# A fused attention and S4 convolution kernel on one core: a new order of work, loads cut into single DMAs, spectra copied whole out of PSUM

## The chip, the core and the metric

The kernel runs on one core of one Trainium2 chip. The metric is the device time of one execution in microseconds (us). Each kernel is timed in several executions and the median is reported; one further execution is profiled. The core has a matrix engine (TensorE; PE in the profile, its weight loads PEld), a vector engine (DVE), an activation engine (ACT), a general engine (POOL) and a sync engine (SP), which issues nearly all of the DMAs here. Each engine works through its own list of instructions in order and waits, where it must, on semaphores that the others raise.

## The reference

Two independent computations share one launch, and their outputs are put side by side.

```
# A: sliding-window attention, S = 2048, D = 576, H = 32 heads of Dh = 18, window W = 256
qkv = x @ wqkv;  q, k, v = split into heads
scores = einsum("bhqd,bhkd->bhqk", q, k) * Dh ** -0.5
mask = (i - j >= 0) & (i - j < W)
p = softmax(where(mask, scores, -1e9))
a = (p @ v, heads concatenated) @ wo
# B: S4 convolution, L = 2048, D = 576 channels, N = 128 states
dt = exp(log_dt);  logdA = dt * (A_re + 1j * A_im);  dB = dt * B
K[d, l] = real(sum_n C[d, n] * exp(logdA[d, n] * l) * dB[d, n])
y = irfft(rfft(pad(u)) * rfft(pad(K)))[:L] + u * Dskip
out = concatenate([a, y], axis=-1)
```

## The kernel before

**Stages.** The work is given to the engines by hand, in four stages that `build` runs one after the other: `front` (loads, scales, the first value and query tiles), `tables` (the taps K of the convolution, beside the rest of the query, key and value projection), `first` (the attention's first groups beside the last taps) and `rest` (attention, convolution and output projection, mixed).

**The order is a table.** `PLAN` holds one string a stage. Each letter names a stream, a Python generator that emits one step of its work when its letter comes up. A letter with a digit emits the work that an earlier step left behind: an evacuation from PSUM, a product, a store. Nothing reorders the steps afterwards, so the position of a letter in the string is the place of those instructions in their engine's list. The letters that matter below:

- `P`: the projection. `G`, `M`, `N`, `R`, `X`: phases, magnitudes, sines, products on POOL and taps; `X4` stores the spectrum of the taps, tile `kst`, to DRAM (`gk`).
- `s`: one step of the pass over the scores for each row's maximum. There are 16 groups of heads and queries (four head groups by four chunks of 512 queries) with 16 such steps in each. A step is 8 matmuls (L844, L852) into a PSUM pair, which a maximum on DVE (`s2`, L878) empties. At the end of a group the maxima are transposed on PE, scaled on DVE, and stored by SP into the query tile as an extra row (`s4`, L871).
- `a`: one score step (L914, L927), ten a group; `a1` is its exponential on ACT (L932), which empties the pair. `v`: one step of the product with the values (L952), ten a group, into the separate pair `po`; `v1` evacuates that, and `n`, `n3`, `n1`, `n6`, `n4` normalise it (DVE, POOL, ACT, POOL) and store it in `od` (SP, L999).
- `k`: load of a tile of spectra of input and taps (`xk`, L672). `c`: 24 steps that transform it (L684) into two PSUM pairs at once. `c1` copies out of these on ACT (L692), `c2` multiplies on DVE (L699), `c3` adds and subtracts on POOL (L704, L705). `d`: the inverse transform (L716), `d1` its copy (L723), `d4` its store. `f`: reload (`hp`, L766). `e`: the last transform (L777). `L`: the loads of Q, K and V of a later group.
- `l`: the output projection's weights and their common scale. The scale goes through DRAM: DVE takes the maximum `om` (L1028), SP stores it (`omx`, L1030) and reads it back over all partitions (`orow`, L1032), and DVE goes on from that (L1034). `w`: the output projection in four chunks (L191 with `woh`); each chunk first reloads its part of `od` into `oh` and `ol`, of which there is one buffer.

**PSUM.** Besides `po`, three pairs of banks (`ring0` to `ring2`) serve every step. The string `SLOTS` says, allocation by allocation in the order of PE's steps, which of the three pairs the step takes. A pair can be taken again only when whatever reads it has read it.

**The spectra step before.** ACT copies the input half of each pair (192 of 384 columns) into `X`. DVE then multiplies `X` with the taps' half, which it reads from the PSUM pairs themselves. So both pairs are held until both products are done.

**DMAs on SP.** SP issues in order, and a DMA that has to wait holds up all behind it. There are eight DMA semaphores in turn, so that a DMA also waits for the one eight places earlier.

## Time and profile before

| | us |
|---|---|
| three timed executions | 870.95, 874.90, 877.46 |
| median | 874.9 |
| profiled execution, its own time | 871.51 |
| its span, first to last instruction | 869.7 |
| busy in the span: PE, DVE, ACT, POOL | 714.5, 599.3, 526.7, 377.8 |
| mean granted clock of PE | 0.928 of full speed |

In the trace the first matmul of the tables starts at 58 us, the first of the attention at 398 us, the first spectra step at 444 us, and the last matmul ends near 866 us. A busy PE is not a PE at its peak, since the ends of matmuls are modelled; what counts is where it stands idle, who ended that idle time, and where the granted clock is at half.

### The profile page before, as it was taken

To read this page: it belongs to the slowest core of one execution; us is meant where nothing else is said; L and a number is where in the kernel's file an instruction comes from. 1 tells how busy PE (TensorE), PEld (TensorE's weight loads), DVE (VectorE), ACT (ScalarE), POOL (GpSimd) and SP (SyncE) were. 2 spreads that over 40 slices of the span, in tenths; PEclk is the share of its full clock that TensorE was granted. 3 is DMA by queue.
4 is the path that set the end of the run, shared out by engine and by line. 5 is a ranking of instruction groups with operands and counts; after the bars stand their busy time and mean duration, and the time that the engine had idled before them with its cause. 6 is when DMAs were issued, how large, how long until landed. Compare 5 with 4: busy or idle time off the path is not lost. (4 is left out here: it accounts for less than half of the span.)

```text
span 869.7 us, 29448 instructions
## 1 busy us (share of the span) xinstructions
PE 714.5 (82%) x12954; PEld 414.7 (48%) x12954; DVE 599.3 (69%) x798; ACT 526.7 (61%) x709; POOL 377.8 (43%) x295
## 2 busy tenths in 40 slices
PE   3675967999889888896887789958998998889977
PEld 2421434456345644464534445425554544457655
DVE  6866887887987787776757798657786779751010
ACT  3247676678777867672455567636676676665421
POOL 2266867766687755565013424312243052432020
PEclk9885969999999999895889999979999999999998
DMA  9795261546347755459457866848549584746843
GB/s 314 266 233 133 63 161 35 142 97 162 83 104 196 150 131 157 100 157 249 100 189 229 268 197 209 212 122 243 180 146 276 170 260 153 216 130 183 245 137 133
DMA packets 211040, 150.74 MB, mean 173 GB/s; under 512 B 102698, under 2 KB 191530, under 8 KB 210656
## 3 DMA queue, kind: packets, MB, share of 16 engines
q1 hardware_dynamic: 208896, 144.87, 59.4%
q0 software_dynamic: 2016, 3.99, 1.5%
q8 instruction: 101, 1.65, 0.8%
q14 instruction: 27, 0.22, 0.1%
HBM read 83.57 MB, written 65.11 MB: 171 GB/s over the span
## 5 line engine op out<-in xcount | busy, mean ns | idle before, releaser
L878 DVE TENSOR_REDUCE m<-ring 128x2 f32<-128x640 f32 (+4 forms) x256 | 186.6, 779 | 52.0 <-PE ring L852 47.9
L932 ACT ACTIVATE P<-ring,esc 128x1024 f32<-128x1024 f32 (+2 forms) x160 | 167.7, 1060 | 83.1 <-PE ring L927 77.0
L559 POOL TENSOR_TENSOR m<-A,tr 128x1024 f32<-128x1024 f32 x72 | 143.9, 2018 | 77.5 <-DVE m L565 66.1
L844 PE MATMUL ring<-K,Q 54*64 54x320 f16 (+4 forms) x1024 | 81.1, 316 | 28.5 <-DMA K<-kz 9.2
L952 PE MATMUL po<-P,V 64*32 64x320 f32 (+4 forms) x2816 | 99.4, 358 | 5.2 <-issue 5.2
L704 POOL TENSOR_TENSOR Y<-t,t 128x384 f32<-128x384 f32 x24 | 24.0, 1001 | 137.5 <-DVE t L699 128.6
L986 POOL TENSOR_TENSOR osb<-osb,T 128x1024 f32<-128x1024 f32 x16 | 37.8, 2363 | 100.4 <-DVE T L981 74.9
L844 PEld LDWEIGHTS <-Q 54*64 54x64 f16 x1024 | 44.0, 108 | 73.8 <-issue 66.8
L914 PE MATMUL ring<-Q,K 55*64 55x320 f16 (+4 forms) x1408 | 65.9, 266 | 15.5 <-ACT P L932 7.0
L191 PE MATMUL pp<-xh,wh 128*128 128x512 f16 x180 | 49.4, 406 | 17.5 <-ACT vst L378 8.2
L994 POOL TENSOR_TENSOR oh<-osb,oh 128x1024 f16<-128x1024 f32 x16 | 34.1, 2131 | 67.5 <-ACT oh L990 67.4
L699 DVE TENSOR_TENSOR t<-X,ring 128x768 f32<-128x768 f32 x48 | 43.5, 946 | 23.8 <-ACT X L692 16.7
L191 PEld LDWEIGHTS <-wh 128*128 128x128 f16 x324 | 32.0, 102 | 55.5 <-issue 18.3
L914 PEld LDWEIGHTS <-K 55*64 55x64 f16 x1408 | 33.3, 108 | 48.2 <-issue 41.2
L565 DVE TENSOR_TENSOR m<-m,m 128x1024 f32<-128x1024 f32 x36 | 53.0, 1472 | 4.8 <-POOL m L559 4.7
L852 PE MATMUL ring<-sm,idb 64*64 64x128 bf16 x896 | 55.1, 222 | 0.6 <-issue 0.6
L588 PE MATMUL ring<-Q,m 128*32 128x64 f32 x2304 | 42.6, 231 | 15.4 <-DVE m L565 13.4
L952 PEld LDWEIGHTS po<-P,V 64*32 64x32 f32 x2816 | 37.8, 106 | 34.0 <-issue 24.1
L588 PEld LDWEIGHTS ring<-Q,m 128*32 128x32 f32 x2304 | 37.0, 117 | 28.7 <-issue 13.0
L191 PE MATMUL pp<-xh,wl 128*128 128x512 f16 x180 | 50.6, 417 | 0.0
L977 DVE STREAM_TRANSPOSE T<-osb 128x1024 f32<-128x1024 f32 x16 | 19.8, 1236 | 42.2 <-ACT osb L962 42.1
L540 POOL TENSOR_TENSOR tr<-tr,mab 128x768 f32<-128x768 f32 x18 | 33.6, 1868 | 30.4 <-ACT tr L535 30.3
(159 smaller groups left out, 1535.6 us busy)
## 6 DMA issues: line engine op xcount, KB each, us to landing
gx<-ust SPq DMA_DIRECT2D x16, 576.0 KB
gk<-kst SPq DMA_DIRECT2D x18, 512.0 KB
xk<-gx SPq DMA_DIRECT2D x24, 384.0 KB
xk<-gk SPq DMA_DIRECT2D x24, 384.0 KB
h<-ho SPq DMA_DIRECT2D x48, 192.0 KB
hp<-h SPq DMA_DIRECT2D x12, 768.0 KB
Q<-qz SPq DMA_DIRECT2D x16, 512.0 KB
K<-kz SPq DMA_DIRECT2D x16, 512.0 KB
```

Of the source, the lines that this page charges most:

```text
L191: self.nc.tensor.matmul(ps, u, v, start=(i == 0), stop=(i == len(ops) - 1))
L559: tt(m[part], A[:, ch, a0:a0 + 8].unsqueeze(3).to_broadcast(sh), tr[:, ch, part, 0:8].unsqueeze(2).to_broadcast(sh), op=OP.mult)
L565: self.nc.vector.tensor_tensor(m[0], m[0], m[1], op=OP.add)
L588: nc.tensor.matmul(kp[32 * st:32 * st + 32, j, :], m[:, ch, 32 * term:32 * term + 32], Q[:, ch, term, :], start=(term == 0), stop=(term == ...
L699: tt(tm, X, pi[i][:, :, 192:384].unsqueeze(2).to_broadcast(sh), op=OP.mult)
L844: nc.tensor.matmul(ps[z:z + 64, b, :n], d["Q"][rr, 2 * b + pp, 64 * qb:64 * qb + 64], d["K"][rr, 2 * b + pp, k0:k1], start=True, stop=Fals ...
L852: nc.tensor.matmul(out, self.idb[rr], self.sm[rr], start=False, stop=True, skip_group_check=True)
L878: self.nc.vector.tensor_reduce(out, x, axis=AX.X, op=OP.max)
L914: nc.tensor.matmul(ps[z:z + 64, b, off:off + w], d["K"][rr, 2 * b + pp, kc:kc + 64], d["Q"][rr, 2 * b + pp, q0:q0 + w], start=(k == 0), st ...
L932: nc.scalar.activation(P[:, :, lo:hi], ps[:, :, lo:hi], AF.Exp, scale=self.esc)
L952: nc.tensor.matmul(po[32 * p:32 * p + 32, z, q0:q0 + w], V[64 * z:64 * z + 64, kb * 76 + 19 * p:kb * 76 + 19 * p + 32], P[p % 2][64 * z:64 ...
L986: nc.gpsimd.tensor_tensor(osb, osb, rb, op=OP.mult)
```

## The change

**The tables of the order.** The strings for `tables`, `first` and `rest` and the string `SLOTS` are all new; `front` is unchanged. The four stages and the arithmetic of all steps except the spectra stay as they are. The number of steps differs only where a DMA is now a step of its own. One line of many:

```
     "rest":
-        "ava1s2ss6ss2s4sss2s2sss2s2ss2sss2s2sss2s2vvsass2aa1a1ss2s2ksvs2sks2aa1ass2ava1a1cc1cc2avv1c1c3a1vvva"
...
+        "ass2s2ss4kskssss2vvs2sasa1a1kvvs2s2vss2s2as2sa1s2s2Laas2s2ssaka1vv1a1a1s2s2vcc1saa1avvLacaka1svs6c2s"
...
 SLOTS = (
-    "0121202102102102102210210120210210210210120121020210120210210201201021020121012021021021021201210201"
...
+    "0122201202112010120102121012012101201020210210120020121021010202012012010201021020211012021010020120"
...
```

**Loads and stores as single DMAs.** The store of the taps' spectrum becomes two DMAs of 256 KB instead of one of 512 KB, each a step of its own. The load of a spectra tile (two DMAs), of a group's Q, K and V (three or four DMAs) and of `hp` (now two halves) were one step each; now every DMA is one step, and other DMAs can stand between them. In all 30 more DMAs are issued.

**Spectra copied whole.** ACT copies all 384 columns of both pairs into a larger `X`, and DVE takes both factors of its products from `X` in SBUF. The pairs are free after ACT's copies.

```
+    def each(self, fn):
+        left, cur = [2], self.cur
+
+        def done():
+            left[0] -= 1
+            if not left[0]:
+                self.cur = cur
+                fn()
         return done
...
-        end = self.both("4", (kst,), lambda: nc.sync.dma_start(gv[:, :, GC * q:GC * q + GC], kst.rearrange("p l s j -> p l (s j)")))
+        def store(l):
+            nc.sync.dma_start(gv[:, l:l + 16, GC * q:GC * q + GC], kst[:, l:l + 16].rearrange("p l s j -> p l (s j)"))
+
+        def stored():
+            for l in (0, 16):
+                self.post("4", (kst,), lambda l=l: store(l))
+        end = self.each(stored)
...
         for m, g in enumerate((self.gx, self.gk)):
+            yield "SP", ()
             nc.sync.dma_start(x[:, :, m], g[8 * t:8 * t + 8, :, :, 192 * ch:192 * ch + 192]
...
         def first():
-            X = fy.tile(sh, F32, name="X")
+            X = fy.tile([128, 2, 2, 384], F32, name="X")
             for i in range(2):
-                nc.scalar.activation(X[:, :, i], pi[i][:, :, :192], AF.Copy)
-            self.post("2", (X, *pi), lambda: second(X))
+                nc.scalar.activation(X[:, i], pi[i][:, :, :384], AF.Copy)
+            self.post("2", (X,), lambda: second(X))
...
             for i, tm in enumerate((t1, t2)):
-                tt(tm, X, pi[i][:, :, 192:384].unsqueeze(2).to_broadcast(sh), op=OP.mult)
+                tt(tm, X[:, :, :, :192].rearrange("p i s j -> p s i j"),
+                   X[:, i, :, 192:].unsqueeze(2).to_broadcast(sh), op=OP.mult)
...
-            self.nc.sync.dma_start(self.hp[m], hv[:, 8 * k:8 * k + 8, 192 * ch:192 * ch + 192])
+            for r in (0, 4):
+                if r:
+                    yield "SP", ()
+                self.nc.sync.dma_start(self.hp[m][:, r:r + 4], hv[:, 8 * k + r:8 * k + r + 4, 192 * ch:192 * ch + 192])
...
         for i in range(3, 16):
-            yield "SP", (), lambda: i - 3 in self.osb
-            self.load(i)
+            for part in self.parts(i):
+                yield "SP", (), lambda: i - 3 in self.osb
+                part()
```

Three places where the order changes follow. The line numbers of the changed kernel are up to 27 higher (L878 is L904 there, L1032 is L1059).

The first place is SP's list between the store of the weights' maximum (`omx`) and its reading back (`orow`), in `rest`. Before:

```order
L1030 DMA omx<-om 128x1
L814 DMA Q_4402<-qz 128x2048
L815 DMA K_4403<-kz 128x4x512
L817 DMA K_4403<-kz 128x4x256
L820 DMA V_4404<-vd 128x912
L999 DMA od<-oh_6831 18x2048 x4
L999 DMA od<-oh_7313 18x2048 x4
L1032 DMA orow<-omx 128x128
```

In the changed kernel:

```order
L844 DMA K_4413<-kz 128x4x256
L1057 DMA omx<-om 128x1
L1026 DMA od<-oh_7118 18x2048 x4
L846 DMA V_4414<-vd 128x912
L1059 DMA orow<-omx 128x128
L788 DMA hp<-h 128x4x192 x2
```

Twelve DMAs stood between the two before: a group's four loads and eight stores of normalised outputs. Now there are five: four such stores and one load.

The second place is DVE's list up to the step that needs `orow` (`og`). Before, from the maximum `om` on:

```order
L1028 TENSOR_REDUCE om<-amxo 128x1
L878 TENSOR_REDUCE m<-ring 128x2
L699 TENSOR_TENSOR t_7915<-X,ring 128x768
L699 TENSOR_TENSOR t_7916<-X,ring 128x768
L878 TENSOR_REDUCE m<-ring 128x2 x10
L1034 TENSOR_REDUCE og<-orow 128x1
```

In the changed kernel, the last ten rows (nine more maxima and a normalisation stand between `om` and these):

```order
L718 TENSOR_TENSOR t_7530<-X 128x768
L718 TENSOR_TENSOR t_7531<-X 128x768
L904 TENSOR_REDUCE m<-ring 128x2
L890 TENSOR_SCALAR m_7581<-ring 32x128
L904 TENSOR_REDUCE m<-ring 128x2
L1004 STREAM_TRANSPOSE T<-osb 128x1024
L1006 RECIPROCAL R<-T 128x32
L1008 STREAM_TRANSPOSE T<-R 128x1024
L904 TENSOR_REDUCE m<-ring 128x2 x6
L1061 TENSOR_REDUCE og<-orow 128x1
```

Eleven maxima and two products stood between `om` and `og`. Now it is 17 maxima, two products and two normalisations. The products no longer name `ring`.

The third place is the end of PE's list, around the third chunk of the output projection. Before, the last value steps (L952) and the last two `e` steps (L777, `x8`) stand ahead of the third chunk, and nothing stands between it and the fourth:

```order
L191 MATMUL ring<-woh,ol 128x288
L952 MATMUL po<-P,V_4396 32x320 x8
L952 MATMUL po<-P,V_4396 32x128 x8
L952 MATMUL po<-P,V_4396 32x64 x8
L952 MATMUL po<-P,V_4396 32x320 x8
L952 MATMUL po<-P,V_4396 32x192 x8
L777 MATMUL ring<-hp,i_5126 64x384 x8
L191 LDWEIGHTS oh
```

In the changed kernel, ahead of the third chunk:

```order
L978 MATMUL po<-P,V_4410 32x320 x8
L978 MATMUL po<-P,V_4410 32x128 x8
L978 MATMUL po<-P,V_4410 32x64 x8
L978 MATMUL po<-P,V_4410 32x320 x8
L978 MATMUL po<-P,V_4410 32x192 x8
L799 MATMUL ring<-hp,i_5206 64x384 x4
L193 LDWEIGHTS oh
```

And between the third chunk and the fourth:

```order
L193 LDWEIGHTS ol
L193 MATMUL ring<-woh,ol 128x288
L799 MATMUL ring<-hp,i_5206 64x384 x8
L193 LDWEIGHTS oh
L193 MATMUL ring<-woh,oh 128x288
```

One `e` step is left ahead of the third chunk, and the last two have moved behind it. Two score steps that stood ahead of the second chunk stand behind it in the changed kernel, in front of those value steps.

More of the change, by code (lines that the diff above doesn't have):

```diff
@@ L141 @@
+    "2102102102102102101202101201201201021020101201201201201021021021020120120120120102102120120201201201"
+    "20120201201201212102101210"
 )
@@ L743, in cload @@
         for n in range(24):
-            yield "SP", (), lambda: n < 2 or n - 2 in self.spd
-            self.conv_load(n)
+            yield from self.conv_load(n)
     def cspec(self):
@@ L966, in aload @@
         for i in range(3, 16):
-            yield "SP", (), lambda: i - 3 in self.osb
-            self.load(i)
+            for part in self.parts(i):
+                yield "SP", (), lambda: i - 3 in self.osb
+                part()
     def norm(self):
```

102 lines of the change are left out of this document (52 added, 50 removed).

## The prediction

> **What bounds the kernel now.** I began with the page's busy shares and the chain that ended last.
>
> ```profile
> PE 714.5 (82%) x12954; PEld 414.7 (48%) x12954; DVE 599.3 (69%) x798; ACT 526.7 (61%) x709; POOL 377.8 (43%) x295
> PE 27%; DVE 7%; DMA 4%; ACT 4%; issue 3%; SPq 1%; ACTq 0%; DVEq 0%
> ```
>
> PE is the engine closest to its limit, and no single line or wait carries the chain; it changes engine every microsecond or two. So the place to look is PE's idle time, by stage (engine busy, then granted clock, DMA share, GB/s):
>
> ```profile
> core 0: us, PE busy (x) PEld busy (x) DVE busy (x) ACT busy (x) POOL busy (x), PEclk, DMA share, GB/s
> 90.00:390.00 300.00, 261.16 (x3420) 150.64 (x3422) 242.90 (x332) 212.44 (x340) 204.92 (x163) 0.94 0.51 125
> 390.00:440.00 50.00, 36.42 (x899) 24.21 (x888) 36.45 (x62) 17.84 (x26) 12.46 (x10) 0.73 0.75 192
> 440.00:810.00 370.00, 317.20 (x7988) 178.63 (x7989) 255.08 (x332) 239.76 (x269) 111.42 (x77) 0.97 0.67 198
> ```
>
> PE is busy 87% in the tables (261 of 300 us) and 86% in the mixed stage (317 of 370). A new order cannot take away PE's work; it has some 39 us of idle time in the tables and 53 in the mixed stage to work on. The table of waits names who ends these in the mixed stage and the tail (total us, times, longest):
>
> ```profile
> PE ring L844 <- DVE m L878: 7.2, 25, 0.5
> DVE og L1034 <- DMA orow<-omx: 7.0, 1, 7.0
> PE ring L914 <- ACT P L932: 7.0, 10, 1.3
> PE ring L191 <- DMA oh<-od: 6.3, 3, 2.5
> PE ring L716 <- ACT P L932: 4.0, 3, 1.4
> PE ring L844 <- ACT P L932: 3.8, 8, 1.3
> ```
>
> Most are waits for a PSUM pair: a step wants `ring` and the exponential (L932) or the maximum (L878) that empties it is not done. The timeline of PE shows such a stretch, a spectra step and what follows it:
>
> ```profile
> 507.47 1.50 PE L684 MATMUL ring<-xk,w 64*32 64x384 f32 x32
> 508.90 0.42 PE L914 MATMUL ring<-Q,K 55*64 55x64 f16 x12
> 509.15 0.28 PE L927 MATMUL ring<-tm,idb 64*64 64x256 bf16 x4
> 510.71 0.33 PE L844 MATMUL ring<-K,Q 54*64 54x320 f16 x4 [1.28 <-ACT P L932]
> 510.84 0.25 PE L852 MATMUL ring<-sm,idb 64*64 64x128 bf16 x4
> 511.02 0.77 PE L952 MATMUL po<-P,V 64*32 64x320 f32 x16
> 511.72 0.42 PE L914 MATMUL ring<-Q,K 55*64 55x64 f16 x12
> ```
>
> While the spectra step's two pairs are held, the one pair left goes from a score step (508.90) to a maximum step (510.71), which idles 1.28 us for the exponential in between. The rows also give step lengths: a maximum step 0.31 us (510.71 to 511.02), a value step 0.70, a score step about 0.4, a spectra step 1.5.
>
> **The change, part by part**, against the profiled execution's own 871.5 us, which is 3.4 us below the median of the timed runs, 874.9.
>
> *The weights' scale through DRAM.* SP, DVE, PE and the stages' clock there:
>
> ```profile
> 561.95 12.10 SPq L999 DMA_DIRECT2D od<-oh  x8
> 574.11 0.34 SPq L1032 DMA_DIRECT2D orow<-omx  x1
> 578.09 0.29 DVE L1034 TENSOR_REDUCE og<-orow 128x1 f32<-128x128 f32 x1 [7.01 <-DMA orow<-omx]
> 579.99 1.54 PE L684 MATMUL ring<-xk,w 64*32 64x384 f32 x16 [4.27 <-DVE m L878]
> 574.50:588.00 13.50, 7.96 (x125) 2.96 (x109) 7.22 (x15) 6.05 (x7) 4.44 (x2) 0.50 0.24 71
> 588.00:602.00 14.00, 12.14 (x373) 7.60 (x372) 11.31 (x16) 10.50 (x10) 1.96 (x2) 1.00 0.82 237
> ```
>
> SP takes 12.1 us over eight `od` stores, then issues `orow`. DVE stands 7.0 us for it with maxima queued behind, PE idles 4.27 in the middle of a spectra step, and then runs 13.5 us at half clock. In the changed order half as many `od` stores stand between (6.1 us at the same pace), and the read-back takes 4.0 (574.11 to 578.09), in sum with the rest some 12 us from `omx` on. From that store DVE has seven maxima and a normalisation to do first, about 8.5 us of work and, at its 69% in this stage (255 of 370), some 12 us. So the wait about vanishes: -7. If it stays whole, 0; if the slow clock goes as well, PE gains what it lacked there (12.14/14.00 x 13.5 - 7.96 = 3.7), -11. Late next is the maximum that feeds PE, which is PE's own pace.
>
> *Spectra copied whole.* What PE waits for the products now:
>
> ```profile
>   PEld ring L716: 3.4, 3
>   PE ring L716: 2.6, 3
>   PE ring L914: 1.8, 4
>   PE ring L844: 1.5, 3
> ```
>
> The three PE rows are 5.9 us (PEld's lies beside them); with pairs that are free before the products run, this goes: -6. What it costs is in these groups:
>
> ```profile
> L692 ACT ACTIVATE X<-ring 128x384 f32<-128x384 f32 x48 | 23.2, 490 | 11.7 <-PE ring L684 7.8 <-DVE T L981 1.5 <-DVE t L699 1.1
> L723 ACT ACTIVATE ho<-ring 128x768 f32<-128x768 f32 x24 | 19.4, 811 | 23.8 <-PE ring L716 22.0 <-DMA xk<-gx 1.7
> L699 DVE TENSOR_TENSOR t<-X,ring 128x768 f32<-128x768 f32 x48 | 43.5, 946 | 23.8 <-ACT X L692 16.7 <-issue 4.8 <-POOL Y L705 2.1
> ```
>
> A copy of 768 elements takes 811 ns by L723, so 48 copies of 811 instead of 490 add 15.4 us to ACT. ACT is busy 65% of this stage (240 of 370), so most hides in its idle time; but exponentials queue behind, and PE waits for these (14.8 us in the three rows above). I take +3, between 0 (all hidden) and +15.4 (all on the path). The products keep their length if DVE reads two SBUF operands as fast as one. The trace has such an instruction, the sum of the tables' products (L565, 1024 elements), once with POOL idle and once behind a POOL product:
>
> ```profile
> 100.74 1.22 DVE L565 TENSOR_TENSOR m<-m,m 128x1024 f32<-128x1024 f32 x1
> 164.07 1.83 POOL L540 TENSOR_TENSOR tr<-tr,mab 128x768 f32<-128x768 f32 x1
> 164.15 2.84 DVE L565 TENSOR_TENSOR m<-m,m 128x1024 f32<-128x1024 f32 x1 [1.36 <-POOL m L559]
> ```
>
> 1.22 alone fits L699's 0.95 for three quarters of the elements; behind POOL it is 2.84, as if DVE had waited for POOL's end at 165.90. L699, with one operand in PSUM, has shown no such stretching. The Trainium skill has this as a rule (SBUF — State Buffer, "Who interferes with whom"): a DVE instruction with two SBUF inputs contends with a GpSimd one that reads SBUF, and the later of the two is blocked. By that rule this edit brings a wait that the old form did not have; the trace agrees, with 2.84 against 1.22.
>
> POOL is busy 30% of the stage (111 of 370). Of 24 pairs of products, 7 would meet it, at up to 1.62 each 11.7 us of DVE time, in an engine that idles 31%: +3 on the path, between 0 and all 24 pairs in full, 39. Sum of the spectra edit: -6 + 3 + 3 = 0, from -6 to +48.
>
> *The order of the steps that take PSUM pairs.* I followed `SLOTS` along PE's list with the step lengths above and counted, in `rest`, pairs that a step wants again before PE has 1.2 us of other work behind a score step (the exponential's 1.1 and its signal): 60 before, 41 now. After maximum steps, with 0.9 us: 67 before, 57 now. These counts are no times; scaled onto the trace's waits, a third of the 14.8 us for exponentials and 15% of the 7.2 for maxima go: -5 - 1 = -6. At worst nothing, since what PE waits for then is the next maximum or exponential, whose engines are as busy as before; at best the pairs' shortfalls halve, -11.
>
> *The tail.* The end of PE's list, the fourth chunk of the projection waiting for its reload, and the last two `e` steps:
>
> ```profile
> 825.24 2.80 PE L777 MATMUL ring<-hp,i 128*64 128x384 f32 x16
> 843.33 0.65 PE L191 MATMUL ring<-woh,ol 128*128 128x288 f16 x4
> 846.51 0.42 PE L191 MATMUL ring<-woh,oh 128*128 128x288 f16 x2 [2.53 <-DMA oh<-od]
> 848.91 0.66 PE L191 MATMUL ring<-woh,oh 128*128 128x288 f16 x2 [1.98 <-DMA oh<-od]
> ```
>
> Between 843.98 and 850 PE has next to nothing to do. The change puts the 2.80 us of `e` there, and score steps into the reload ahead of the third chunk, in the place the `e` left: -3. If the reload is late behind the `hp` load now queued ahead of it on SP, 0; if the earlier gap shrinks too, -5.
>
> *Tables, `first` and the split stores.* The engines' work in the tables is the same, and the same count of hurried pairs comes out alike before and now, so I take 0. An order that is new over 300 us can do better or worse by a good part of its 39 us of PE idle time: -12 to +15. Issuing 30 more DMAs costs SP about half a microsecond each, by the 0.34 of `orow`'s row 10 us, on a queue that mostly waits for others: 0.
>
> Sum: -7 + 0 - 6 - 3 + 0 = -16, so 855.5 for a profiled execution, and in the ratio of 874.9 to 871.5 **859 us** for the median.
>
> **The rivals.** *The gain is eaten on DVE and by the next wait.* The product pairs meet POOL more often than by chance, say 15 of 24, because POOL's normalisations follow DVE's transposes in bursts: 15 x 1.62 = 24 us on DVE, half of it ahead of maxima that PE wants, +12 instead of +3; and released pairs only move PE's wait to the next exponential, -1 instead of -6. That is 855.5 + 9 + 5 = 869.5, a median of 873: no change. For it: DVE's 2.84; both engines near PE's pace. Against it: DVE idles 115 of 370 us here. This is also what the rule of the skill amounts to where it holds fully.
>
> *SP blocks (slower).* Each load now stands in SP's list by itself, among the stores of the maxima row `Q<-m` that ten score steps of a group wait for. One load that waits for PE or a buffer ahead of such a store stops SP, as the `od` stores did for 12.1 us. An event of that kind cost 7.0 of DVE's time and 3.7 of slow clock, about 11. Two such events would more than use up the 16 us of the forecast; three give 855.5 + 33 = 888.5, four 899.5. I price it at three, a median of 892. For it: 51 load steps where there were 13. Against it: the waits are for steps far back on PE, and splitting lets SP put a store between two loads.
>
> *The tables gain as well.* Taps come at more even distances in the new list, and POOL, DVE and PE each idle less: the -12 above, 843.5, a median of 847.
>
> **How the numbers follow.** This kernel's measurement tells about 1% from no change, so faster means under 866 and slower over 884. The forecast as worked out has a chance of 0.47, with its own range from 849 to 869 (the wait for `orow` kept or its clock won too, plus the tables by a few); nine tenths of that is faster, the rest within 1%. The tables' gain has 0.12, eaten gains 0.23, blocked SP 0.18, of which a little stays under 884. Faster: 0.42 + 0.12 + 0.03 = 0.57; slower 0.17; same 0.26. The range leaves out the far end of the blocked case and of the tables' gain: 840 to 884.
>
> **What would show it.** In the changed kernel's profile: the wait of `og` for `orow` under 2 us and no half-clock stretch after it; no PE wait ended by the products, copies of 0.81 us on ACT; products at 0.95 us, with some up to 2.4 where a POOL instruction runs; the waits of PE for L932's successor at about 10 us instead of 14.8; 1.4 us `e` steps between the last two chunks, and the gap before the fourth down to 3 us. I am wrong if the products' mean is over 1.4 us, if SP stands over 8 us ahead of a `Q<-m` store while PE idles, or if the start of the attention, at 398 us before, has moved by more than 10 us: then the tables decide, and not these terms.

## The result, and the profile after

The changed kernel takes 843.25 us (median of 4 runs, 832.45 to 846.52), beside 875.22 us for the kernel before. The ratio is 0.956, with a 95% interval from 0.946 to 0.966; it goes by the runs within 1.5% of the fastest of their kernel (832.45 and 840.61 here), while the two medians stand at 0.963. A second measurement of the same pair gave 842.78 and 0.964 (0.960 to 0.969). So it is some 32 us faster by the medians where 16 were forecast, and its profiled execution (846.52 us, span 844.7) is the slowest of its four runs. A second profile of it, 845.45 us, reads the same.

The busy times of the page's first line changed little. In the chain that ended last PE's share rose from 27% to 40%:

```profile
PE 709.5 (84%) x12954; PEld 412.5 (49%) x12954; DVE 594.6 (70%) x798; ACT 534.1 (63%) x709; POOL 380.9 (45%) x295
PE 40%; DVE 10%; ACT 9%; DMA 8%; SPq 4%; issue 4%; POOL 0%; ACTq 0%; DVEq 0%
```

The time went in the mixed stage. Here is the work cut at the same places of the program, in windows: first the kernel before (from its first spectra step to the first matmul of the output projection, and from there to the end), then the changed one (tables, and the same two).

```profile
444.30:780.60 336.30, 284.35 (x7438) 156.64 (x7423) 249.96 (x327) 218.44 (x246) 105.03 (x73) 0.97 0.67 198
780.60:869.70 89.10, 77.78 (x916) 55.02 (x915) 6.51 (x7) 33.37 (x39) 12.97 (x7) 0.95 0.56 172
```

```profile
90.00:390.00 300.00, 260.80 (x3422) 149.90 (x3418) 240.26 (x333) 218.26 (x352) 209.96 (x164) 0.95 0.53 127
443.70:750.80 307.10, 274.19 (x7262) 151.33 (x7253) 245.72 (x322) 220.31 (x239) 99.34 (x69) 0.99 0.70 210
750.80:844.70 93.90, 83.96 (x1049) 57.88 (x1041) 10.22 (x12) 38.10 (x44) 19.37 (x11) 0.96 0.57 177
```

The first spectra step starts at 443.7 instead of 444.3. From there on PE idles 42.9 us (32.9 and 9.9) instead of 63.3 (52.0 and 11.3), and is busy 358.2 instead of 362.1. That is the whole difference of the two traces. PE is busy for less time because less of it runs at half clock, and because 57 matmuls, most of them of value steps, now stand ahead of the first spectra step (4665 matmuls start before it instead of 4608).

The waits of the changed kernel on PE (its L870 and L940 are L844 and L914 of before, L736 is L716, L711 is L692, L958 and L904 are the exponential and the maximum):

```profile
PE ring L870 <- DMA K<-kz: 11.0, 3, 6.1
PE ring L193 <- DMA oh<-od: 5.5, 3, 2.7
PE ring L870 <- ACT P L958: 4.8, 13, 0.7
PE ring L870 <- DVE m L904: 4.7, 17, 0.5
PE ring L940 <- DVE m L904: 3.9, 15, 0.4
PE ring L940 <- ACT P L958: 2.4, 6, 0.6
PE ring L940 <- ACT X L711: 2.3, 4, 1.2
PE ring L736 <- ACT P L958: 0.2, 1, 0.2
```

Of the first row 6.1 us fall at the start of the attention, as 7.2 did before. No row names the products, but score steps now wait 2.3 us for the copies, which end their hold on the pairs. The three rows for exponentials are 7.4 us where the same three were 14.8, and the longest is 0.7 where it was 1.4. The timeline of PE at a spectra step shows one place where such waits are gone. A maximum step, a score step and an inverse step follow behind it, each in a PSUM pair, without a gap, where one pair had to do before:

```profile
509.16 1.69 PE L703 MATMUL ring<-xk,w 64*32 64x384 f32 x32
510.77 0.33 PE L870 MATMUL ring<-K,Q 54*64 54x320 f16 x4
510.93 0.23 PE L878 MATMUL ring<-sm,idb 64*64 64x128 bf16 x4
511.00 0.41 PE L940 MATMUL ring<-Q,K 55*64 55x256 f16 x8
511.22 0.25 PE L953 MATMUL ring<-tm,idb 64*64 64x128 bf16 x4
511.40 0.56 PE L978 MATMUL po<-P,V 64*32 64x64 f32 x32
511.90 1.53 PE L736 MATMUL ring<-Y,i 32*64 32x192 f32 x32
```

In the 4.5 us from the start of each of the 24 spectra steps PE idled some 21 us in all before, and 7 now. Outside these stretches, from the first spectra step on, it went from 42 to 36 us. Part of that is a row that no term of the prediction held: ahead of value steps PE idled 5.2 us for nothing that the profile shows, and now 0.2. The groups of the spectra step:

```profile
L711 ACT ACTIVATE X<-ring 128x768 f32<-128x768 f32 x48 | 36.8, 810 | 12.5 <-PE ring L703 9.9 <-issue 1.7
L718 DVE TENSOR_TENSOR t<-X 128x768 f32<-128x768 f32 x48 | 44.2, 961 | 12.2 <-issue 10.4 <-ACT X L711 1.6 <-POOL Y L725 0.2
```

The copies take 0.81 us. The products take 0.96, and only one of the 48 is stretched (1.54 us). DVE no longer stands for the copies either, 1.6 us in place of 16.7: in the new order 13 of the 24 pairs of products start 1.7 to 10.8 us behind the copies, and 11 within 0.9.

### The profile page after: what moved, and what is told of

Read it like the earlier page. It is cut to its first block, busy times and chain, and to the rows that moved or that the text cites. A ratio compares the mean times of both kernels' runs of the same rounds, so it can differ in the third digit from the quotient of the medians.

```text
span 844.7 us, 29482 instructions
## 1 busy us (share of the span) xinstructions
PE 709.5 (84%) x12954; PEld 412.5 (49%) x12954; DVE 594.6 (70%) x798; ACT 534.1 (63%) x709; POOL 380.9 (45%) x295
## 4 chain that ended last, share of the span: by engine, by line
PE 40%; DVE 10%; ACT 9%; DMA 8%; SPq 4%; issue 4%; POOL 0%; ACTq 0%; DVEq 0%
PE ring L193 7%; PE po L978 6%; DVE m L904 6%; PE pp L193 5%; PE ring L736 4%; PE ring L870 4%; PE ring L940 3%; DMA K<-kz 3%; ACT P L958 3%; PE ring L703 3%; PE ring L600 1%; PE ring L799 1%; PE ring L490 1%; PE ring L478 1%; ACT ring L512 1%
## 5 line engine op out<-in xcount | busy, mean ns | idle before, releaser
L904 DVE TENSOR_REDUCE m<-ring 128x2 f32<-128x640 f32 (+4 forms) x256 | 188.5, 777 | 62.7 <-PE ring L878 51.2
L958 ACT ACTIVATE P<-ring,esc 128x1024 f32<-128x1024 f32 (+2 forms) x160 | 166.1, 1059 | 77.0 <-PE ring L953 70.7
L870 PE MATMUL ring<-K,Q 54*64 54x320 f16 (+4 forms) x1024 | 79.7, 313 | 26.6 <-DMA K<-kz 11.0
L870 PEld LDWEIGHTS <-Q 54*64 54x64 f16 x1024 | 40.6, 108 | 73.3 <-issue 64.0
L940 PE MATMUL ring<-Q,K 55*64 55x320 f16 (+4 forms) x1408 | 64.2, 264 | 10.5 <-DVE m L904 3.9
L193 PE MATMUL pp<-xh,wh 128*128 128x512 f16 x180 | 52.5, 427 | 21.1 <-ACT vst L390 8.7
L878 PE MATMUL ring<-sm,idb 64*64 64x128 bf16 x896 | 54.1, 221 | 0.3 <-issue 0.3
L940 PEld LDWEIGHTS <-K 55*64 55x64 f16 x1408 | 33.6, 108 | 40.5 <-issue 37.7
L718 DVE TENSOR_TENSOR t<-X 128x768 f32<-128x768 f32 x48 | 44.2, 961 | 12.2 <-issue 10.4
L512 ACT ACTIVATE ring<-ring 128x1024 f32<-128x1024 f32 x36 | 36.6, 1017 | 14.3 <-PE ring L490 12.5
```

The lines of the kernel that those rows point to most:

```text
L193: self.nc.tensor.matmul(ps, u, v, start=(i == 0), stop=(i == len(ops) - 1))
L512: self.nc.scalar.activation(m, m, AF.Exp)
L718: tt(tm, X[:, :, :, :192].rearrange("p i s j -> p s i j"), X[:, i, :, 192:].unsqueeze(2).to_broadcast(sh), op=OP.mult)
L870: nc.tensor.matmul(ps[z:z + 64, b, :n], d["Q"][rr, 2 * b + pp, 64 * qb:64 * qb + 64], d["K"][rr, 2 * b + pp, k0:k1], start=True, stop=Fals ...
L878: nc.tensor.matmul(out, self.idb[rr], self.sm[rr], start=False, stop=True, skip_group_check=True)
L904: self.nc.vector.tensor_reduce(out, x, axis=AX.X, op=OP.max)
```

## The experiments

### One part alone, in the old order

`b_whole` makes only the spectra edit in the kernel before.

```
-            X = fy.tile(sh, F32, name="X")
+            X = fy.tile([128, 2, 2, 384], F32, name="X")
...
-                nc.scalar.activation(X[:, :, i], pi[i][:, :, :192], AF.Copy)
+                nc.scalar.activation(X[:, i], pi[i][:, :, :384], AF.Copy)
...
-                tt(tm, X, pi[i][:, :, 192:384].unsqueeze(2).to_broadcast(sh), op=OP.mult)
+                tt(tm, X[:, :, :, :192].rearrange("p i s j -> p s i j"),
+                   X[:, i, :, 192:].unsqueeze(2).to_broadcast(sh), op=OP.mult)
```

> The kernel before, with nothing changed but the spectra step: ACT copies all 384 columns of both pairs, and DVE takes both factors from SBUF. The old order stays, so the products still stand close behind the copies. Theory 1 (the gain comes from the order of rest, the spectra edit is worth nothing by itself, as the prediction summed it: -6 +3 +3): 875 us, 871 to 880. Some 10 of the 24 pairs of products meet a POOL instruction there (they overlapped one in 11 steps of the old trace), and these are up to 1.6 us longer. Theory 2 (the released pairs are the gain): 866 or less, with the 5.9 us of PE waits for the products gone. Theory 3 (collision of DVE and POOL is what makes the edit dear unless the order avoids it): over 884, with a mean of the products over 1.4 us.

Measured: 888.33 us, ratio 1.017 (1.012 to 1.023). The edit alone costs 13 us by the medians. The group of its products, and the row of its waits that grew most (L845 is the maximum step, L879 its maximum):

```profile
L699 DVE TENSOR_TENSOR t<-X 128x768 f32<-128x768 f32 x48 | 60.4, 1299 | 28.5 <-ACT X L692 21.0 <-issue 5.3 <-POOL Y L706 2.1
```

```profile
PE ring L845 <- DVE m L879: 20.2, 30, 3.3
```

One collision in the timeline, with DVE's, POOL's and PE's rows in order of time:

```profile
483.50 3.71 DVE L699 TENSOR_TENSOR t<-X 128x768 f32<-128x768 f32 x2
...
484.07 2.32 POOL L995 TENSOR_TENSOR oh<-osb,oh 128x1024 f16<-128x1024 f32 x1 [1.16 <-ACT oh L991]
...
486.36 3.06 POOL L987 TENSOR_TENSOR osb<-osb,T 128x1024 f32<-128x1024 f32 x1
487.14 0.81 DVE L879 TENSOR_REDUCE m<-ring 128x2 f32<-128x640 f32 x1
488.00 0.33 PE L845 MATMUL ring<-K,Q 54*64 54x320 f16 x4 [3.35 <-DVE m L879]
```

Eight of the 24 pairs meet POOL, all at a normalisation (seven were forecast by chance), and are some 2.1 us longer each (60.4 less 43.5 in all). This pair takes 3.71 us, two times 0.95 without POOL, and ends 0.8 us behind the end of POOL's first normalisation, whose successor is then stretched in turn (3.06 us, where the group's mean was 2.36 in the kernel before). The maxima stand behind the pair, and PE idles 3.35 us. The rule of the Trainium skill that the prediction weighed (SBUF — State Buffer, "Who interferes with whom") says that the later of two such instructions is blocked; the trace agrees, on both engines. Theory 3 is nearest by the time; the products' mean, 1.30 us, stayed under its 1.4. That the collisions are what the 13 us consist of is not shown by this run; `b_pool` below takes them away.

`b_split` keeps the old spectra step and the old order, and cuts the loads and stores into single DMAs as the change does; in the strings each `k`, `f` and `X4` is doubled, and each `L` stands three or four times.

```
-        ...s2s2ksvs2sks2aa1a...
+        ...s2s2kksvs2skks2aa1a...
```

> The old order and the old spectra step, but every load and store of the change is a DMA step of its own; the steps stand next to each other, so SP's list is the same but for 30 more DMAs. Theory 1 (the split alone does nothing; it only lets an order put something between): 875 us, 872 to 879. A theory that smaller DMAs alone land earlier and so end waits: 870 or less.

Measured: 873.87 us, 0.9985 (0.9956 to 1.0013). Single DMAs alone do nothing that these runs can tell.

`b_lrow` moves one letter, so that `orow` is issued right behind `omx`.

```
-        ...s4aasfvs2kla1a1slvs2v1Ln4n4cc1c2elsve1...
+        ...s4aasfvs2kla1a1sllvs2v1Ln4n4cc1c2esve1...
```

> The kernel before, with one letter of the rest string moved: SP issues the read-back of the weights' scale (orow) straight behind its store (omx), ahead of the eight od stores and the group's loads. All else stays. By the prediction's term: 7.0 us of DVE's wait go and up to 3.7 of slow clock: 864 to 868 us. The rival is that this wait only moves: SP now stands about 2 us for omx to land, and the third engine in line (ACT, which waited 6.1 us for the od stores beside it) sets the same end: 873 to 877.

Measured: 872.87 us, 0.9986 (0.9959 to 1.0012): nothing, as the rival had it. DVE's 7.0 us are gone from its profile, but the queue of SP and the list of ACT show what was waiting beside it:

```profile
561.93 0.33 SPq L1030 DMA_DIRECT2D omx<-om  x1
569.40 0.33 SPq L1032 DMA_DIRECT2D orow<-omx  x1
569.82 0.68 SPq L814 DMA_DIRECT2D Q<-qz  x1
...
580.76 1.06 ACT L990 ACTIVATE oh<-osb 128x1024 f16<-128x1024 f32 x1 [6.43 <-DMA od<-oh]
```

SP now stands 7 us for the 512 bytes of `omx` to land, the `od` stores come behind, and ACT, which needs `oh` back from these stores, idles 6.43 us with the exponentials behind it.

### The new rest with the old tables

`h_newrest` has the old strings for `tables` and `first` (with the doubled letters, and `ava1s2ss6ss2sss` from the start of the old `rest` behind them), the new one for `rest` with its names, and all other edits.

> The old tables and first, the new rest with its PSUM pairs, the split DMAs and the whole-copied spectra. (What the old first did less than the new one, five score steps and a few more, stands in the old order ahead of rest.) Theory 1 (all of the gain is made in rest, and the tables are worth nothing): 843 us, 836 to 850, as the changed kernel. If the new tables take part in it by more even distances of their steps: 850 to 858.

Measured: 847.86 us, 0.971 (0.965 to 0.976), some 5 us above the changed kernel, which intervals that overlap don't settle. From its first spectra step, at 449.8 us, to its end it takes 396.9 us; the changed kernel takes 401.0 and the kernel before 425.4. So the gain is made in `rest`, as theory 1 said.

### The changed kernel again, and its products moved forward

`a_again` is the changed kernel. `a_near` moves 18 of the 24 `c2` in `rest` to straight behind their `c1` (two of them four and ten steps behind). `a_near_old` is the same list with these 18 steps in the old form.

```
-        ...ans6c1s2ssvs2sa1aa1s2kvc2sn3a...
+        ...ans6c1c2s2ssvs2sa1aa1s2kvsn3a...
```

```
+OLD = (0, 2, 3, 6, 7, 8, 9, 12, 13, 14, 16, 17, 18, 19, 20, 21, 22, 23)
...
-                nc.scalar.activation(X[:, i], pi[i][:, :, :384], AF.Copy)
+                w = 192 if n in OLD else 384
+                nc.scalar.activation(X[:, i, :, :w], pi[i][:, :, :w], AF.Copy)
...
-                   X[:, i, :, 192:].unsqueeze(2).to_broadcast(sh), op=OP.mult)
+                   (pi[i][:, :, 192:384] if n in OLD else X[:, i, :, 192:]).unsqueeze(2).to_broadcast(sh), op=OP.mult)
```

> The changed kernel itself once more, as the measure for the three others on the same chip: 843 us, 832 to 847 as before. In the traces so far every half-clock stretch of PE starts and ends on a grid of 3.413 us that is at another place in each run, and follows a piece of that grid in which PE stood idle for about half or more. If that is what spreads the times by 1.6%, this run has its grid elsewhere and with it one or two half-clock stretches more or fewer after 440 us, and the same idle times of PE.

> The changed kernel with the products of 18 of the 24 spectra steps moved forward in DVE's list, to straight behind ACT's copies (two of them four and ten steps behind), as the old order has them; all else stays. In the trace of the changed kernel POOL is busy in that place for 5 of the 18. Theory 1 (the new order lets the edit be free because the products lie where POOL is idle): 4 or 5 products are some 2 us longer and DVE's maxima late by that, 847 to 853 us. Theory 2 (the place of the products doesn't matter, the released pairs alone do): 843.

> The same list as the one with 18 products moved forward, but these 18 steps in the old form: ACT copies half the columns, the products read the other half from PSUM, and both pairs are held until then, some 1.9 us longer. Theory 1 (the gain of rest is that steps behind a spectra step find free pairs; PE's idle time in the 4.5 us from the start of each spectra step fell from 20.8 to 7.2 us): 18 of 24 steps get back 0.4 to 0.6 us each and more where the new naming uses the pair at once, so 7 to 15 us over the kernel with the whole copies, no stretched products: 850 to 860. Theory 2 (only the order of score and maximum steps matters): within 3 us of the changed kernel.

Measured: 842.78 us (838.45 to 851.17) for `a_again`, with PE's idle time after 440 us at 43.5 us beside 43.6 and 10.7 us of half clock beside 13.3. `a_near` takes 900.82 us, 1.031 (1.026 to 1.036), and `a_near_old` 892.23, 1.022 (1.018 to 1.027). Both theories fall for `a_near`: 58 us more, and not from POOL, since the products' mean is 1.05 us. Its waits (L721 is the products, L714 the copies, L907 the maximum, L873 and L943 maximum and score steps):

```profile
DVE t L721 <- ACT X L714: 30.3, 13, 6.9
PE ring L873 <- DVE m L907: 27.6, 22, 6.4
PE ring L943 <- DVE m L907: 20.3, 18, 4.7
```

DVE works in order. A product that stands early in its list makes DVE wait for ACT's copy, 30.3 us instead of 1.6, and PE waits 47.9 us for the maxima behind it instead of 8.6. And at that place the old form is better by 9 us, not worse: its copies are 0.32 us shorter, and DVE's wait for them is 23.9 us. Both theories for `a_near_old` fall too. So whole copies gain nothing where the products follow at once; they leave the pairs free while the products stand elsewhere, which is what the new list does. The whole new list with the old form was not run, since by the lists its engines would wait for each other in a circle: products stand behind maxima of steps that need the pairs which the products hold. So what the whole copies are worth within the new list is argued and not measured.

### Products moved back in the old order

In `b_late_all` the products of most steps of `b_whole` (19, not 20 as the expectation says) stand behind up to three maxima, in one case four, with POOL's sums moved along where they would come first. `b_late_names` has the same list with the pairs of `rest` named anew.

```
-        ...nvvn3aa1kcc1aa1dc2sad1s2sksvs2s2a1v1cc...
+        ...nvvn3aa1kcc1aa1dsad1s2sksvs2s2c2a1v1cc...
```

> The old order with whole-copied spectra, as in b_whole (888 us), but the products of 20 of the 24 steps moved back in DVE's list behind up to three maxima (four in one case; four steps where a later spectra step or the inverse needs them at once stay); the old PSUM names stay. In b_whole 8 pairs of products met POOL and were 2 us longer each, and DVE stood 28.5 us ahead of products, most for ACT's copies, with maxima queued behind. Theory 1 (it is the place of the products that makes whole copies dear or cheap): both go, 866 to 876, the products' mean below 1.0 us. Theory 2 (the copies themselves, 0.32 us longer each on ACT, are what costs): 883 to 890.

> The same list with the PSUM pairs of rest named anew: each step takes the pair that is free longest, counted along PE's list with the step lengths, and with a spectra step's pairs free after the copies. Counted that way, the steps of rest come 27.8 us too early for their pairs with the old names and 15.4 with these. Theory 1 (the old names keep using the one pair that was left while the products held the others, so that whole copies need new names to be worth anything): 8 to 14 us less than with the old names, and PE's idle time in the 4.5 us behind the start of a spectra step falls from 18 to 8 us or less. Theory 2 (names matter little, since PE then waits for the next exponential): within 3 us.

Measured: 907.57 us, 1.040 (1.035 to 1.045), and 896.05, 1.025 (1.020 to 1.030). Both theories for `b_late_all` fell: the products were back to 1.04 us and DVE's wait ahead of them fell from 28.5 to 10.4 us, but the time rose by 19. In the traces PE's idle time after 440 us grew from 69.3 to 84.9 us. New waits are 9 us of that (L717 is the inverse step):

```profile
PE ring L717 <- POOL Y L705: 7.6, 4, 3.0
PE ring L717 <- POOL Y L706: 1.6, 4, 0.4
```

The inverse steps stood where they had stood, and PE now waited for POOL's sums. Most of the rest are waits for maxima. Moving one step of a chain asks for moving the next too. The names gave 11.5 us, as theory 1 had it, and the idle time behind spectra steps fell from some 22 to 11 us, not to 8.

### Collisions and names apart, in the old order

`b_pool` changes only POOL's list in `b_whole`: at seven places `c3` goes to straight behind its `c2`, and at four of them `n3` from ahead of it to behind. `b_whole_names` changes only `SLOTS`. `b_pool_names` does both.

```
-        ...s2s2nvvn3aa1kcc1aa1dc2sad1s2sksvs2s2a1v1...
+        ...s2s2nvvaa1kcc1aa1dc2c3n3sad1s2sksvs2s2a1v1...
...
-    "1021021021201210210212010210210210021021021201202102102102102102102010212012012010210210210210201201201"
+    "1021021021021021021021021021021021021021021021021021021021021020120120120120120120120120120120120121021"
```

> b_whole (888 us: old order, whole-copied spectra) with nothing moved but seven additions of spectra (c3) and four normalisations on POOL: at the seven places where products met a normalisation on POOL, POOL now does that step's addition first, for which it has to wait for the products, and the normalisation after it. PE, DVE and ACT keep their lists. Theory 1 (the collision is the price of the edit: 16 us on DVE, of which PE's waits for maxima rose from 6.6 to 20.4 us): the products are back at 0.95 us each and the time falls by 10 to 14, to 874 to 878. Theory 2 (the longer copies on ACT are): 884 to 888.

> b_whole with only the PSUM pairs of rest named anew, for pairs that are free after the copies (the count of shortfalls goes from 27.8 to 15.4 us). In the list with postponed products the same edit gave 11.5 us. Theory 1 (the old names give the released pairs nothing to do): 8 to 12 us less than b_whole, 876 to 880, and the idle time behind spectra steps falls from 18 to 10 us or less. Theory 2 (names gave something there only because that list was bad): within 4 us of 888.

> Both: no collisions with POOL, and new names. Theory 1 (the two effects are apart, and add): 888 - 12 - 11 = 865 us, 861 to 869; so the spectra edit with names that use it would be worth some 10 us even in the old order, and the rest of the new order 20 more. Theory 2 (PE's waits only move from one to the other): 873 to 878.

Measured: 886.80 us, 1.015 (1.010 to 1.020); 885.35, 1.012 (1.005 to 1.019); 878.00, 1.004 (1.001 to 1.008). Each alone did what it should in its own place: the products' mean is 0.955 us in the first, the idle time behind spectra steps 8.5 us in the second. But they gave only 1.5 and 3 us, which is within the noise of these runs (4 to 6 us on each time), and by their times both single edits came out as their second theories. So the collisions by themselves are not the 13 us. Both together gave 10 us, which is clear of the noise, and came out at the edge of their second theory, 873 to 878. Whether the two effects add is not shown. With both, the row of the products, the largest wait of PE on a maximum and the stage from 440 us on read

```profile
L699 DVE TENSOR_TENSOR t<-X 128x768 f32<-128x768 f32 x48 | 44.3, 963 | 30.6 <-ACT X L692 22.8 <-issue 5.7 <-POOL Y L706 2.1
PE ring L845 <- DVE m L879: 13.1, 26, 1.8
440.00:875.00 435.00, 372.79 (x8412) 218.01 (x8410) 257.55 (x334) 265.69 (x286) 118.29 (x80) 0.94 0.63 191
```

The edit without its collisions and with names that use it is 3 us above the kernel before. The other 35 us, from 878 to 843, came only with the new order. They do not lie behind the spectra steps: there PE idles 7.5 us here and 7.3 in the changed kernel. Elsewhere, from the first spectra step on, it idles 54.1 us here, 42.2 in the kernel before and 35.5 in the changed kernel. In the old order, then, freeing the pairs behind a spectra step did not shorten the kernel; other waits grew by nearly as much, such as that of maximum steps for maxima, from 7.2 us to the 13.1 above.

### What was left in the changed kernel

`a_oh2` gives the reload of the attention's output two buffers. `a_omx` moves three letters of the weights' scale (store, read-back, DVE's step) some 15 us back; two of them leave the line below, and all three come back further on. `a_both` does both.

```
-        ...ass6aa1c3ls2vn1n4vaaa1Lla1dvfsa1...
+        ...ass6aa1c3s2vn1n4vaaa1La1dvfsa1...
...
-            for n, b in (("cc", 1), ("fs", 2), ("fy", 1), ("wo", 1), ("wo2", 1), ("wor", 2), ("wy", 2)):
+            for n, b in (("cc", 1), ("fs", 2), ("fy", 1), ("wo", 1), ("wo2", 2), ("wor", 2), ("wy", 2)):
```

> The changed kernel with two buffers instead of one for the reloaded output of the attention (oh and ol): the reload of a chunk need not wait for the chunk before it to be read. PE stood 2.7 us ahead of the third chunk and 2.3 + 0.5 ahead of the fourth, with a half-clock stretch of 6.8 us behind the last. Theory 1 (the buffer is what the reload waits for): these go, 5 to 9 us less than the changed kernel, 834 to 838. The rival: the reload waits for the od stores of the last groups, which SP issues among others until 811 us, and the wait only moves: 841 to 845.

> The changed kernel with three letters moved: the store of the weights' maximum (omx), its reading back (orow) and DVE's step on it come some 15 us later in rest. In the three traces of the changed kernel PE stands 4.1 us near 540 us for a load of K that takes 13 to 14 us to land and has the 512-byte store omx just behind it, with a half-clock stretch after it; orow was issued 12.8 us after omx. Theory 1 (that store, 128 pieces of 4 bytes, holds up the DMA queues and K with them): stall and half-clock stretch go, 837 to 840 us. The rival (the load of K is late because Q, K, V and hp are issued within 7 us and share the DMA engines): the stall stays, 842 to 845.

> The changed kernel with both edits: three letters of the weights' scale later, and two buffers for the reload of the attention's output. If the first takes 4 to 6 us and the second, as measured, 1 to 2 (its waits were gone, but 2.2 us of another came in their place): 835 to 838 us. If neither does anything: 843.

Measured: 841.45 us, 0.964 (0.959 to 0.968); 841.24, 0.963 (0.959 to 0.967); 836.83, 0.959 (0.954 to 0.963). By its time the first is its rival's, though the reload's waits did go, as theory 1 said: 1.0 us of them is left, and 2.2 us of a wait for a pair stand beside it. In the second the profile is as theory 1 said, with no stall near 540 us and no half-clock stretch between 440 and 832 us, but the median is only 1.5 us lower, which is within the noise. Both together are the fastest kernel of this study, at 0.959 of the kernel before where the changed kernel measured in the same way has 0.964; the intervals overlap, so it is not shown to be faster.

## Why the prediction was wrong

The direction came out, and so did most of the signs that it named: the waits, the copies and the products. A half-clock stretch is still there at the read-back, though. The size did not come out, and two steps above all failed. The cost of the whole copies was put at 6 us, which canceled their gain, and did not arise; and the gain of the order of the pairs was sized by who ended PE's idle time. Together these two were put at -6 us, and in the mixed stage PE's idle time fell by 19. Two further terms, the weights' scale and the clock, were off as well. All sizes here are from the two traces, which are 25 us apart; the medians are 32 apart because the profiled run of before lay 3.7 us below its median and that of after 3.3 above.

**Whole copies, summed at -6 + 3 + 3 = 0.** The -6 was nearly right: PE's waits for products were 5.9 us and are gone, with 2.3 us of waits for copies in their place. The two +3 were the error in the new order. No delay of exponentials by ACT's longer copies shows (PE's waits for these fell), and the products meet POOL once, not seven times. "7 would meet it" treated the place of a product as chance; in a list written for this edit it is chosen. In one stretch of the changed kernel the copies end at 469.1 us, POOL normalises from 472.1 to 474.5, and the products stand at 476.7. In the old order, where place was chance, the count was nearly right (8) and a pair cost 2.1 us of DVE's time instead of 1.62. The edit as a whole cost 13 us there and not 0; which part of it is the collisions' own is open, since taking them away alone gave 1.5 us.

**The order of the pairs, -6.** The rule "a third of the 14.8 us for exponentials and 15% of the 7.2 for maxima" gave -5 and -1. Exponentials gave -7.4; maxima, in the rows of the maximum and score steps, fell from 9.3 to 8.6. The rows quoted then held a larger thing: the 1.28 us ended by an exponential at 510.71 came while the spectra step held the two other pairs. Counting idle time by who ended it hid that some 21 us of it lay behind spectra steps, of which 14 went. That is 14 of the 20 us by which PE's idle time fell from the first spectra step on. But `b_pool_names` has the same 14 and is no faster than the kernel before, so they count only in a list that does not lose them elsewhere.

**The weights' scale, -7.** DVE's wait did vanish, as forecast:

```profile
L1061 DVE TENSOR_REDUCE og<-orow 128x1 f32<-128x128 f32 x1 | 0.3, 276 | 0.0
```

But taken away alone it was worth nothing: in `b_lrow` ACT waited for the same stores in its place. And the forecast set 12 us of DVE's work against 12 us until the read-back lands; neither sum was right. DVE had 14 maxima, two products and a normalisation to do behind `omx`, not seven maxima and a normalisation, and reached `og` 24.3 us behind it. The four `od` stores took SP 1.5 us and not 6.1, and it stood for `omx` itself. That both came later, and DVE by more, was luck. In the changed kernel SP still stands ahead of `orow`, for 8.6 us, and PE at the same time for a load of K:

```profile
525.02 0.58 SPq L842 DMA_DIRECT2D K<-kz  x1
525.65 0.82 SPq L844 DMA_DIRECT2D K<-kz  x1
526.51 1.45 SPq L1057 DMA_DIRECT2D omx<-om  x1
528.01 1.48 SPq L1026 DMA_DIRECT2D od<-oh  x4
530.36 0.35 SPq L846 DMA_DIRECT2D V<-vd  x1
539.30 0.34 SPq L1059 DMA_DIRECT2D orow<-omx  x1
```

```profile
539.21 0.33 PE L870 MATMUL ring<-K,Q 54*64 54x320 f16 x4 [4.17 <-DMA K<-kz]
```

So in place of PE's 4.27 us of before stand 4.17, for another reason. What was won there is clock: 3.4 us at half clock follow in place of 13.7. This is close to a sign that was to prove the prediction wrong, SP standing for over 8 us ahead of `Q<-m` stores while PE idles: four of these stores stand two loads behind `orow`. The rival of a blocked SP came true here once instead of three times, and not by a load; moving the stall away gave 1.5 us (`a_omx`), not the 11 that the rival put on each.

**The clock, not a term of its own.** It was priced only at `orow` (3.7 us at best). Half-clock stretches after 440 us went from 31.0 to 13.3 us (the last one of a trace runs past the last instruction), and PE's busy time fell by 4.7 us, in part with them. In `b_whole` they rose to 58.8 us. Its trace is 17.1 us longer than that of before: 4.1 lie ahead of the first spectra step, in work that the edit leaves alone; behind it PE is busy 9.0 us longer and idle 4.0 us longer. So a wait on PE of a few microseconds can be paid twice.

The rest stood. Tables 0: the attention starts 0.5 us earlier in these two traces. Over all traces it starts at 400.7 us in the mean with the old tables (10 traces, 397.5 to 402.5) and at 399.0 with the new (7 traces, 397.1 to 401.0), so they may have given some 1.6 us. Single DMAs 0: `b_split`. The tail -3 came to -1.4 by PE's idle time from the first projection matmul on; the `e` steps cover a part of the reload of the fourth chunk (2.8 us of waits are left of 4.5), and the gap ahead of the third, 2.69 us, is 0.9 longer than it was:

```profile
804.48 0.28 PE L193 MATMUL ring<-woh,oh 128*128 128x288 f16 x1 [2.69 <-DMA oh<-od]
...
817.80 2.80 PE L799 MATMUL ring<-hp,i 128*64 128x384 f32 x16
...
823.45 0.66 PE L193 MATMUL ring<-woh,oh 128*128 128x288 f16 x2 [2.31 <-DMA oh<-od]
```

The rival of a gain eaten on DVE described the edit in the old order well (a collision with POOL's normalisations, maxima behind), and the new order avoids it. The rival whose number came nearest, tables that gain too (847 us), was right for no reason that it gave.

What stays open is how the 35 us between `b_pool_names` and the changed kernel divide among the lists of the engines. By the traces 18.3 us are idle time of PE after 440 us (61.9 to 43.6) and 11.7 its busy time, with 37.7 us less of half clock and the 57 matmuls that stand earlier. No single list was shown to hold them, and the two placings of the products tried by hand made things worse.

## What to carry to other kernels

An edit that frees a resource earlier is worth what the order around it makes of that: the same copies cost 13 us in the old list and are part of a gain of 32 in a list written for them, so a term summed part by part in the old order, collisions by chance included, is no bound for a new one. Before a wait is booked as gained, list every engine that waits for the same transfer or the same queue at that moment, and group PE's idle time by what holds its buffers, not only by who ended it; and when one group goes, look whether the others grew, as in `b_pool_names`. And price a stall of PE with the clock: its own length, and up to half of the stretch at half clock behind it.

## What the runs showed of the hardware

**The clock follows windows on a fixed grid.** In all 17 traces the stretches of half clock begin and end on a grid of 3.413 us, to within 2 ns over a whole run, which lies at another place in each run. I took every grid window after 445 us in which PE ran at full clock and counted how often the next was at half clock, by the share of the window in which PE was idle:

```
PE idle in the window   windows   next at half clock
under 30%                  1672       0
30 to 40%                    94       6
40 to 50%                    61      19
50 to 60%                    30      22
60% and more                 53      53
```

From half clock it came back after 102 of 109 windows with less than 10% idle, and after 2 of 62 with more. So a PE that is idle for half a window mostly loses the next, and then nearly always has to be busy for nine tenths of one. The Trainium skill (TensorE: Matmul & The Clock Gate, "HAM oscillation — how this bites in real kernels") warns of gaps of PE over some 3.4 us. Here 2.05 us of idle time in one window, 60% of it, were enough each time, and the measurement decides. Since the grid's place differs from run to run, the same waits can cost a window more or less: in the two traces of the changed kernel the stretch near 540 us is 3.4 us long in one and 6.8 in the other. Whether that is all of the spread of its runs (838 to 851 us in the second measurement) was not shown.

**A store of 512 bytes kept its reader waiting for 7 to 13 us.** `omx` is written as 128 pieces of 4 bytes. The wait is for this store and not for the DMA eight places earlier: in the changed kernel that one, a load of K, had landed whole at 533.0 us, and the last part of `omx` landed at 539.24, just ahead of `orow` at 539.30. The read-back behind it could be issued 7.5 us later in `b_lrow`, 10.1 in `a_omx`, and 12.8 in both traces of the changed kernel. In the second trace of that kernel PE even stopped for 6.22 us within a score step, between the ninth and the tenth of twelve matmuls, with nothing that it is shown to wait for:

```profile
540.04 0.38 PE L940 MATMUL ring<-Q,K 55*64 55x128 f16 x9
546.64 0.27 PE L940 MATMUL ring<-Q,K 55*64 55x64 f16 x3 [6.22 <-issue]
```

With the store moved 15 us back, beside loads that nothing waits for at once, no stall of that size is left in either trace (`a_omx`, `a_both`).

The traces also show that slow loads move with the store. In the changed kernel's first trace the loads of K after 440 us land within 4.0 to 8.6 us, but the one issued just ahead of `omx` takes 13.4. In `a_omx` the two loads of K at the old place take 6.8 and 6.9 us, and the two beside the moved store, 10.5 and 9.6, are the slowest of its trace. That speaks against the rival of its expectation, that the load was late because others were issued close to it. In the second trace of the changed kernel, though, the loads beside `omx` took 6.9 and 7.7 us, and PE stopped elsewhere. That the store's small pieces hold up what is queued with them fits most of this, but how they do it no run here shows.
